# A new order of TensorE, ScalarE, VectorE and store instructions in a fused attention and feed-forward kernel on one core

## The chip, the core and the metric

The kernel runs on one core of a Trainium2 chip. A core has five engines with an instruction queue each: TensorE (PE in the profile, with its weight loads shown apart as PEld), ScalarE (ACT), VectorE (DVE), GpSimd (POOL) and SyncE (SP). Each engine takes its own queue in order, and semaphores make an instruction wait for work on another engine. TensorE writes its products to PSUM, and ScalarE or VectorE move them from there to the on-chip memory. DMA transfers are started by POOL's and SP's queues. The metric is the time of one execution on the device in microseconds.

## The reference

Eight batches b of 12 heads, 448 positions, 64 values a head. The attention has no softmax: scores are clipped at zero and squared. Its output is the input of a feed-forward layer with an exact GELU. Inputs and output are float32.

```python
scores = scale * np.matmul(q, k.transpose(0, 1, 3, 2))     # scale = 1 / sqrt(64)
attn = np.maximum(scores, 0.0) ** 2 / S                    # S = 448
attn_out = np.matmul(attn, v)                              # (8, 12, 448, 64)
x = attn_out.transpose(0, 2, 1, 3).reshape(B * S, H * D)   # (3584, 768)
h = x @ w_in                                               # w_in (768, 2048)
g = 0.5 * h * (1.0 + erf(h * inv_sqrt2))
out = g @ w_out                                            # w_out (2048, 768)
```

## The kernel before, in words

**Attention.** The 12 heads make three groups g of four. For each batch and group the kernel needs transposed keys (kT) and queries (qT). For the first two batches TensorE makes them: a TK step (L620) or a TQ step (L648) transposes into a PSUM bank `tp`, and one copy on ScalarE (L521) or VectorE (L519) brings the bank to kT or qT. For the later batches SP's queue makes them with transposing DMAs (L675), from natural-order data that POOL's queue loads (L472 to L477 for queries, L556 and L559 for keys, L579 for values, L492 to L494 and L498 for the two weight matrices). A QK step (L752) multiplies one block of 64 keys or two of them with the queries of four heads into a PSUM pair `ps`. Its relu follows on ScalarE (L769) or VectorE (L771), which empties the pair into a tile `a_sq`; the square of that tile is on VectorE (L781) or ScalarE (L779). When the seven key blocks of a group are squared, an AV step (L831) multiplies them with the values into a PSUM pair `pav`, and two copies empty it into xT, the transposed attention output. In the first batch, attention works in halves of 224 query columns, named a and b here, so that the pairs of the 128x896 relus hold two half blocks.

**Feed-forward.** Two forms of the first product exist. For the earliest part, psh steps (L891, with the GELU at L901) multiply xT by `win_sb` directly. For the rest, F1 steps (L1048) use a scheme with seven block products in place of eight, on sums of weight blocks (`ws`, L962), sums of activation blocks (`t_x`, L1007) and partial sums added by VectorE (L1086), with the GELU at L1098; FB steps (L1199) are the same for the last batch. The second product (F2, L1375) uses the same scheme, adds its parts at L1409, and the finished rows of 128 tokens go to the output by SP's queue (L1328).

**What sets the order.** Every step is registered as one `Op` in a list (`sch.open`), in an order that the program fixes. A string `ORDER` (L83 to L175, 1618 words) then names all of them once, in the order in which they are issued. The letter of a word is the engine: P and Q for TensorE, A for ScalarE, D for VectorE, G for POOL, S for SP; the number is the index in the list; Zn is a product of zeros over n columns on TensorE (L1677) that does nothing but fill time. `Scheduler.place` takes the words one by one:

```python
for word in ORDER.split():
    if word[0] == "Z":
        op, eng = next(fills), "PE"
    else:
        op, eng = self.open[int(word[1:])], names[word[0]]
        if word[0] == "Q":
            op.split()
    ...
    self.commit(max(self.ready(op), free), op, eng, dur, lat)
```

Since each engine has its own queue, only the order of the words of one engine among themselves, and the order in which words ask for buffers, reaches the chip. The number next to a QK step's is its relu and the one after that its square (P33, 34, 35); the two after an AV step's are its copies to xT (P45, 46, 47); the one after a TK or TQ step's is its copy (P17, 18).

**Buffers.** A step takes a buffer where its word stands and waits until an earlier owner has been read. There are three PSUM pairs (`w`), for QK, AV and F1 steps, two single PSUM banks (`f`), for TK, TQ, psh, fill and F2 steps, and 14 tiles `a` for relu outputs and partial sums. A word with Q in place of P takes the two single banks in place of a pair, and its relu becomes two instructions of half the size.

**Names that the text uses.** P14 and P17 are TK steps of batch 0, group 0 and P11 is its TQ step; P19 and P23 are the TK steps of groups 1 and 2. P33, P36, P39 and P42 are the first QK steps. P45, P60 and P72 are the AV steps of half a, P87, P99 and P114 those of half b. P165, P168, P171, P174, P198, P207 and P213 are QK steps of batch 1. P141 and P143 are the first two psh steps, P258 the first F1 step. P225 is an AV step of batch 1 and P375 an F1 step that reads its xT. P299 is the first QK step of batch 2. S1612 and S1613 are the last two stores (L1328): S1612 stores 256 of the last right half's 384 columns and S1613 the remaining 128.

Of the kernel before, what the change touches and what calls it, by code (L numbers as in the profile page):

```python
# [100 lines left out]
D423 P428 D456 D426 P459 A427 A424 D440 G234 A419 P311 P317 P445 P461 A441 D453 D449 D457 A318 D460  # L101
S230 S231 P463 P323 D312 A429 A381 A446 A313 D462 S232 P308 D316 S233 D301 A324 D309 D464 P350 P465
D466 A351 D352 P305 P302 A306 D310 P335 A307 P467 G237 G149 G152 G155 D458 D336 D468 A303 D304 P469
D470 P326 A327 P365 A366 P341 A342 D319 P471 P338 G239 G292 A339 A340 P320 D491 D472 A321 P332 A322
D337 D492 D343 G293 G294 D493 A333 P329 G295 D330 D367 S475 S476 P495 G296 A496 P497 P353 D498 P359
D334 D360 A331 A354 P362 A363 P499 S473 A500 P501 P356 P347 D325 A364 D328 P344 A357 A358 D355 D348
G297 D361 D345 D346 D349 G481 P511 A512 P520 A521 P503 P517 D502 A518 P526 P368 A369 D527 A519 P514
D504 S477 S478 G484 D494 S479 S480 P529 P505 D370 D583 P587 A513 P604 P507 D584 D515 G298 P594 A530
G487 A588 P589 A595 D605 D586 D522 A528 P607 P590 D508 D585 D592 P611 A516 P606 D608 A591 G482 G483
D621 D609 P599 A612 G485 G486 P596 S657 D531 P613 G488 D600 A601 S658 G489 S510 P623 P640 G663 D597  # L110
D614 P616 D617 A610 A641 A624 D622 P602 D506 P619 P625 P642 A593 A615 A603 A620 A598 Q523 D628 D645
A524 A646 P535 P626 P643 D525 S509 A536 A627 P630 P647 P538 A539 D631 D644 Q532 D533 A618 A534 P571
A572 P632 D648 P649 D673 P635 Q550 P553 A554 P652 D650 A651 D633 P638 P655 A656 D551 D674 A639 D636
A637 P677 P577 D653 A654 P559 A560 P547 S659 P679 D552 D675 P565 D548 S660 A678 D680 A578 A555 D540
P562 D563 D537 A566 S661 A567 D676 P681 P683 A682 D684 A634 P541 P574 P544 A545 D546 A629 A564 G666
P685 D686 S474 D542 D543 D693 D694 G490 P687 D688 S691 P689 D690 P568 A575 A549 A569 P556 D695 P719
A557 A558 A720 P713 D714 P697 D698 P725 A726 A727 A576 P728 D729 P722 D696 A570 P699 S692 D700 P731
P737 D732 P701 D702 D723 P703 P705 P746 D579 S662 G669 G664 G665 A561 D573 A747 P580 G667 A581 D704
D706 D730 D582 D785 P716 P709 A717 D710 S712 G668 G670 D786 P789 D788 G671 P806 A724 D790 P791 D794
D807 A738 P796 P813 D814 P707 A718 D787 A733 D715 P808 A739 D811 D708 A721 A812 P809 P792 D823 A810  # L120
P749 A750 Q734 D793 P740 A741 A795 D797 P798 P815 D816 P818 D819 D799 A742 A735 A736 D748 P825 P842
A843 P801 P821 P804 A751 A805 Q770 D802 P752 S711 A822 D826 P828 P845 A846 P832 D824 D753 D829 P849
D875 P827 S859 S860 S861 P844 D754 A850 P854 A800 S862 P834 P851 A771 A803 P879 D855 D830 D852 A833
D835 D847 P837 A817 A820 A853 P840 P857 P764 D876 D838 P755 D765 D877 A880 P883 A756 D878 A836 A858
A831 P773 A774 P761 D762 P881 D882 A841 G865 G868 A848 A884 P743 A763 A839 P767 D768 P918 D766 A775
P885 D886 P887 G672 D757 D888 A744 A856 A919 D745 P889 D890 D772 S893 P933 A934 D895 A935 P758 A759
D896 P779 A780 P776 A777 S863 A760 P891 P899 A900 S864 D898 P945 P927 D892 A778 P921 A922 A928 D946
D781 A947 P903 D920 P901 D897 P942 P948 A949 D769 D943 P782 A783 P924 G871 D902 A904 P930 D929 D931
D932 A925 P905 D906 A784 P907 D908 G866 P951 P915 D923 P939 D987 P909 G867 A940 D926 G869 G870 G872
D910 D988 P911 D912 S914 A952 P991 P1008 A916 A917 D990 Q963 D964 D944 P957 G873 A953 S1061 A958  # L130
D959 P936 A937 Q954 A938 P998 P1015 D992 P993 P1010 D1009 S1062 D989 A999 D950 P1011 A1016 A955
D1013 A1014 A956 P994 D996 P1003 D1012 A995 P1020 P1027 D1025 P1044 P1000 D1021 A1022 D1004 D1028
A1045 D1001 P1029 A997 P1046 D1049 A1050 D1032 A1005 P1030 P1047 D1026 P1017 D1018 A1031 P1034 P1051
D1048 S1063 S1064 S1065 A1002 P1023 P1036 P1053 D1052 D1054 A1035 D1037 P1039 P1056 P1006 G1067
A1007 G1070 D1057 D1079 A1024 P1042 P1059 A1060 P1081 D1040 S913 P978 A1041 A1043 A1058 P1117 D941
A979 P960 A961 D1077 D1078 D1118 P1150 D1151 S894 D962 P1120 P1083 A1121 P966 P972 A1082 P969 A973
P1085 P1141 D980 D967 D1084 A970 D1086 A968 D974 D1080 P981 A982 G874 A1055 P975 P1087 D1088 D1142
P1089 A1033 D1090 A976 P1091 A983 A1019 D1092 A1038 P1144 P1132 D1097 D977 P1147 A965 D971 A1133
A1148 D1134 P1093 P1101 D1094 S1095 S1066 P1129 A1130 P984 A1119 P1126 D1099 D1098 P1103 A985 A986
D1102 P1105 D1104 D1127 A1106 A1145 P1107 P1135 A1131 P1123 P1156 A1124 D1122 P1109 D1143 P1195  # L140
G1073 G1068 A1125 D1136 A1157 P1193 D1189 P1212 G1069 G1071 G1072 D1137 A1149 S1263 P1210 D1108
D1110 P1111 D1100 P1113 G1074 D1128 A1211 D1215 P1165 A1194 G1075 D1198 D1112 S1115 A1199 A1166
# [1572 lines left out]
```

## Time and profile before

| what | value |
|---|---|
| median of three runs | 359.96 us (359.49 to 360.23) |
| profiled execution, its own time | 360.24 us |
| its span in the profile | 358.5 us |
| TensorE busy | 350.0 us in 3841 matmuls |
| VectorE busy | 305.6 us in 515 instructions |
| ScalarE busy | 270.3 us in 437 instructions |
| POOL busy | 102.9 us in 138 instructions |
| DMA moved | 43.01 MB, mean 120 GB/s |

All times in the profile count from the start of the span. A row of a timeline has the start, the length from the start of its first instruction to the end of its last, the engine and line, the operation with output and input, the tile mode for TensorE, the sizes, and the number of instructions that the row joins; in brackets stands the idle time of the engine before it and what ended this. Instructions of one engine overlap by part of their length, so what a step costs its engine is read as the distance between starts. In the digit strip the span is cut in 40 slices of 9.0 us, and each digit is the busy share in tenths.

### The profile page before, as it was taken

How to read it: one execution, taken by the hardware profiler on the slowest of the kernel's cores; microseconds unless marked ns; L12 is line 12 of the kernel's file. 1: busy time of each engine (PE TensorE's matmuls, PEld its weight loads, DVE VectorE, ACT ScalarE, POOL GpSimd, SP SyncE). 2: the span in 40 equal slices, each digit the busy share in tenths (PEclk: the TensorE clock that was granted, in tenths of full speed). 3: DMA queues.
4: the chain of work that ended last, by engine and by line, in shares of the span. 5: the costliest groups of instructions: out<-in, count | busy, mean ns of one | idle time of the engine just before them, and what ended most of it. 6: DMA issues, size and time to landing. Idle time of an engine off the chain costs nothing.

```text
span 358.5 us, 9223 instructions
## 1 busy us (share of the span) xinstructions
PE 350.0 (98%) x3841; PEld 248.0 (69%) x3841; DVE 305.6 (85%) x515; ACT 270.3 (75%) x437; POOL 102.9 (29%) x138
## 2 busy tenths in 40 slices
PE   8879999999999999999999999999999999999995
PEld 3557679955588655896557965579668855788663
DVE  2999999999997989988889898779988998595762
ACT  3999997899869896978978669789986778334300
POOL 8664816096193104700075100841000000000000
PEclk9999999999999999999999999999999999999999
DMA  9999999999999958995399941998402001012222
GB/s 171 197 201 204 201 204 157 146 145 148 183 141 146 214 84 127 154 169 79 63 90 159 214 69 51 88 171 209 72 3 90 2 0 46 3 44 90 88 87 91
DMA packets 124361, 43.01 MB, mean 120 GB/s; under 512 B 102688, under 2 KB 120992, under 8 KB 124320
## 3 DMA queue, kind: packets, MB, share of 16 engines
q0 software_dynamic: 85328, 22.47, 66.2%
q1 hardware_dynamic: 38448, 19.50, 26.0%
q8 instruction: 30, 0.49, 0.5%
q10 hardware_dynamic: 544, 0.46, 0.4%
q14 instruction: 11, 0.09, 0.1%
HBM read 45.61 MB, written 11.01 MB: 158 GB/s over the span
## 4 chain that ended last, share of the span: by engine, by line
PE 92%; ACT 5%; DVE 2%; issue 0%; DVEq 0%; ACTq 0%
PE pso L1375 37%; PE pe L1048 30%; PE ps L752 9%; PE pav L831 8%; PE pb L1199 4%; ACT a_sq L769 3%; PE psh L891 2%; PE spin L1510 1%; DVE a_sq L781 1%; DVE a_sq L771 1%; ACT xT L521 0%; PE tp L620 0%; PE fill L1677 0%; ACT a_sq L779 0%; ACT qT L521 0%
## 5 line engine op out<-in xcount | busy, mean ns | idle before, releaser
L769 ACT ACTIVATE a_sq<-ps 128x896 bf16<-128x896 f32 (+1 forms) x125 | 106.7, 893 | 14.5 <-PE ps L752 14.2
L781 DVE TENSOR_TENSOR a_sq<-a_sq 128x896 bf16<-128x896 bf16 (+1 forms) x108 | 63.8, 615 | 2.1 <-ACT a_sq L769 1.9
L1375 PEld LDWEIGHTS <-s_sb 128*128 128x128 bf16 x456 | 42.4, 98 | 32.3 <-issue 7.1
L1048 PEld LDWEIGHTS <-win_sb 128*128 128x128 bf16 x624 | 59.5, 98 | 2.7 <-issue 1.5
L771 DVE TENSOR_SCALAR a_sq<-ps 128x896 bf16<-128x896 f32 (+1 forms) x57 | 55.5, 988 | 2.6 <-PE ps L752 2.2
L779 ACT ACTIVATE a_sq<-a_sq 128x896 bf16<-128x896 bf16 x61 | 57.2, 959 | 0.5
L752 PE MATMUL ps<-qT,kT 64*64 64x448 bf16 (+1 forms) x756 | 49.7, 337 | 2.7 <-ACT a_sq L769 1.3
L1098 ACT ACTIVATE h_sb<-part 128x448 bf16<-128x448 f32 x78 | 43.2, 580 | 9.9 <-DVE part L1086 9.7
L1086 DVE TENSOR_TENSOR part<-pe,part 128x448 f32<-128x448 f32 x78 | 45.5, 620 | 5.3 <-PE pe L1048 3.6
L1375 PEld LDWEIGHTS <-h_sb 128*128 128x128 bf16 x336 | 31.9, 98 | 22.9 <-issue 4.0
L1048 PEld LDWEIGHTS <-ws 128*128 128x128 bf16 x468 | 44.1, 98 | 3.5 <-issue 2.9
L1375 PE MATMUL pso<-wout_sb,s_sb 128*128 128x384 bf16 (+2 forms) x232 | 41.1, 321 | 0.0
L1375 PE MATMUL pso<-t_sb,s_sb 128*128 128x384 bf16 x224 | 41.1, 327 | 0.0
L1375 PE MATMUL pso<-wout_sb,h_sb 128*128 128x384 bf16 x224 | 41.1, 327 | 0.0
L559 POOL DMA_DIRECT2D nk<-in_k_dram x36 | 34.7, 968 | 9.6 <-DMA wout_sb<-in_moe_w_out_dram 8.1
L831 PE MATMUL pav<-a_sq,v_sb 64*64 64x448 bf16 (+1 forms) x756 | 36.5, 329 | 0.8 <-DVE a_sq L781 0.8
L752 PEld LDWEIGHTS <-kT 64*64 64x64 bf16 x756 | 19.6, 105 | 23.7 <-issue 17.7
L1048 PE MATMUL pe<-t_x,win_sb 128*128 128x224 bf16 x312 | 34.5, 259 | 0.0
L1048 PE MATMUL pe<-xT,win_sb 128*128 128x224 bf16 x312 | 34.1, 259 | 0.0
L1048 PE MATMUL pe<-t_x,ws 128*128 128x224 bf16 x312 | 33.2, 259 | 0.0
L521 ACT COPY part<-pe 128x448 f32<-128x448 f32 x53 | 26.4, 541 | 8.9 <-PE pe L1048 6.2
L1409 DVE TENSOR_TENSOR osb<-pso,p_sb 128x384 f32<-128x384 f32 x42 | 23.3, 554 | 9.4 <-PE pso L1375 5.9
(74 smaller groups left out, 409.5 us busy)
## 6 DMA issues: line engine op xcount, KB each, us to landing
out_dram<-osb SPq DMA_DIRECT2D x19, 384.0 KB, 2.8
nq<-in_q_dram POOLq DMA_DIRECT2D x38, 112.0 KB, 5.8
nk<-in_k_dram POOLq DMA_DIRECT2D x36, 112.0 KB, 5.8
v_sb<-in_v_dram POOLq DMA_DIRECT2D x5, 672.0 KB, 7.6
v_sb<-in_v_dram POOLq DMA_DIRECT2D x9, 224.0 KB, 8.0
win_sb<-in_moe_w_in_dram POOLq DMA_DIRECT2D x8, 192.0 KB, 9.2
wout_sb<-in_moe_w_out_dram POOLq DMA_DIRECT2D x4, 384.0 KB, 12.7
wout_sb<-in_moe_w_out_dram POOLq DMA_DIRECT2D x1, 1536.0 KB, 15.8
```

What stands on the lines that cost most here:

```text
L521: A.copy(dst, src)
L559: nc.gpsimd.dma_start(nk[b][:, g0, :, e], rows[:, e].rearrange("p (i d) -> p i d", d=D))
L752: nc.tensor.matmul(side(ps, e)[64 * j : 64 * j + 64, x * w : x * w + w], kT[r, g, i * 128 + 64 * j : i * 128 + 64 * j + 64], moving, start ...
L769: A.activation(to, x, AF.Relu, scale=c_att)
L771: V.tensor_scalar(to, x, c_att, 0.0, op0=mybir.AluOpType.mult, op1=mybir.AluOpType.max,)
L779: A.activation(ar, ar, AF.Square)
L781: V.tensor_mul(ar, ar, ar)
L831: nc.tensor.matmul(side(pav[0], e)[o2 : o2 + 64, :w], vt[b][r, 2 * g + e, bass.ts(i, D)], box["a2"][r, e, o : o + w], start=(i == 0), stop ...
L1048: nc.tensor.matmul(bank[name][:, y, z * HS : z * HS + HS], w[:, k, bass.ts(mm, 128)], right()[:, k], start=first and k == 0 and z == 0, st ...
L1086: V.tensor_add(get(to), ps(name), get(other))
L1098: A.activation(h_ring()[:, m : m + 2, o + half[c].start : o + half[c].stop], src().rearrange("p (x n) -> p x n", x=2), AF.Gelu,)
L1375: nc.tensor.matmul(box[bank][:, n0:n1], left()[:, kf], right()[:, kf, n0:n1], start=bool(need) and kf == 0, stop=kf == K2 - 1, skip_group_ ...
```

## The change

The string `ORDER` is written anew. It names the same 1618 operations, each once. Each engine keeps its number of words; 87 operations move from VectorE to ScalarE and 87 others from ScalarE to VectorE. POOL's words keep their order. The orders of TensorE, ScalarE, VectorE and SP differ. On TensorE, the first 74 places hold the same set of steps in both strings, in another order; after that (from P258) the orders differ locally. P39, P159, P225 and P550 are Q words before and P words after, and P72, P171 and P1117 from P to Q. On SP, 45 of the 67 words stand in another place, stores against transposing DMAs from batch 3 on, and at the end S1613 stands before S1612. Nothing else in the program is changed. The first lines, the line with Q299, and the last lines of both strings:

```diff
@@ -81,94 +81,94 @@
 ORDER = """
-G0 G1616 G1 G3 G4 G7 D13 Z1024 A10 G118 A16 G2 P14 D15 P11 D12 P17 D18 P19 D20 P42 A43 P36 A37 P33
-P21 D44 D22 P23 A24 D34 P51 P25 A52 D26 P48 Q39 D35 G117 P54 A49 D40 P63 A64 D55 P57 P27 D28 P29 D30
-P69 P66 A58 D59 P31 D32 A70 D71 A67 G121 G6 G125 D38 P90 P93 D41 A94 D65 P131 A132 P102 A103 P129
-P45 A46 A47 G126 Z672 A91 P84 D130 Q159 D50 D68 P72 G5 A160 D85 G8 G122 A73 G120 P111 A112 A53 D56
-D74 P75 P133 D76 P156 D113 A157 A134 P81 D82 P139 A140 P60 D61 D83 P96 P108 D62 A97 D109 P137 P78
-A79 D86 D80 P174 A175 D77 D92 P135 A136 D95 G124 P171 A172 D104 D98 P87 A88 P105 D89 A106 P168 A169
-P141 A142 P162 D107 D110 D138 P195 A163 P99 D100 Q114 G119 P207 D101 D176 P165 A196 A115 D116 A158
-P198 A199 D173 P143 A144 D208 D170 A166 D197 P240 A241 A161 D250 D251 P180 D181 D167 G128 G123 G9
-D164 P222 A223 P192 P242 A243 P244 D253 D209 P145 A193 A146 P213 A214 A245 D194 P177 A178 D200 P189
-A179 P183 D215 D190 D191 P246 A184 A247 P210 D182 A211 P216 P186 A187 D185 P248 A249 P258 P275 A217
-D254 G127 G236 D188 P219 A276 G235 G238 G147 A220 Q201 D224 D212 D255 G148 P204 A202 A203 A205 D252
-A221 P260 P277 A206 D259 P261 P278 A262 D409 D280 D218 D257 P265 D256 P282 A283 A266 Q225 A279 D412
-D263 P270 P267 A226 A227 D371 D372 P284 D268 A269 P287 D285 P375 A264 A281 P392 A393 P273 G150 D271
-P290 D288 P382 P399 D447 D374 A376 P378 P395 A274 D373 D450 A289 A291 D448 G151 P377 D451 P394 D397
-A286 A400 A383 P387 P404 D380 A396 A379 P384 A272 D405 A406 P401 D388 P413 P430 A389 A414 A431 D385
-A386 P420 P437 A421 D402 S228 A438 P407 D452 P390 D410 P416 A391 D411 P433 A408 D455 P442 S229 D454
...
-A417 A434 P415 A398 G153 G154 P432 D443 A444 D435 A436 D418 P422 P439 A403 Q299 A300 P314 A315 P425
...
-D1586 S1588 P1593 P1595 A1594 D1596 P1597 A1598 S1609 P1599 D1592 P1601 D1600 P1603 D1602 P1606
-S1610 D1604 S1611 P1605 D1607 S1612 D1608 S1613
+G0 G1616 G1 G3 G4 G7 D13 Z1024 A10 G118 P14 D15 G2 G117 G121 G6 P11 A16 P17 D12 P33 A18 P36 A37 G125
+D34 G126 P39 A40 P21 D22 P19 D20 P42 A43 P23 A24 D35 D38 P54 P48 A49 P25 D26 P57 A58 D41 Z672 D44
+P69 P27 D55 P29 A70 P66 D59 A30 P51 D28 A67 D52 G5 G8 P93 P31 P131 A94 D68 D132 P90 D32 A91 G122
+G120 G124 G119 G128 P63 A64 P84 D85 P129 A130 D65 P45 P133 D71 A46 A47 P108 P75 D134 A109 P78 A79
+D53 D76 Q72 A73 A74 D110 G123 G9 P102 A103 D50 P111 A112 P159 A160 G127 D56 P81 D82 A77 P139 D140
+P60 D95 D86 A61 A62 P156 A157 P137 P96 P141 D138 D104 A97 D98 A80 P168 P105 D83 A106 P135 D136 P87
+A142 A169 D92 D88 D89 P162 D113 Q171 A172 A163 D107 P174 P99 A100 D175 D170 D176 A101 Q114 A115 D116
+P195 D250 A196 D161 P213 A214 D215 P165 A166 D167 P143 A144 P240 P180 D158 A181 D173 A241 D197 P192
+A193 D164 P198 A199 D252 P244 A245 P242 D251 P222 D223 P207 A208 D182 A243 P177 A178 G236 P189 A200
+P183 A184 A179 P248 A249 D224 D190 D191 P246 A247 P186 P219 A220 G235 P210 A211 G238 G147 G148 D253
+P145 D209 P258 A146 D187 P275 G150 P216 D185 A212 D188 D194 Q201 A217 A259 D221 D254 D255 P204 A276
+A205 P260 P277 D257 A202 A218 D206 G151 D280 P261 D263 A281 D256 P265 P278 A279 P282 D266 P225 A262
+P267 P284 D409 D203 A283 A226 A227 P375 A376 P287 S228 S229 P270 D285 A286 D268 A269 P273 P290 A291
+D371 D372 P392 D288 A393 D271 D374 A272 P382 D412 A274 P399 G153 G154 P378 A400 P395 A289 D373 S230
+S231 S232 D450 D451 A383 P377 P394 D397 P387 A379 D388 A396 D380 P384 A381 A264 G234 P401 D402 D385
+A386 P404 D405 D410 D411 P413 P430 A431 P390 A414 D447 A391 P420 P437 A438 P407 G237 A408 D448 A421
...
+D449 P416 P433 A434 P415 S233 P425 A417 D426 P432 D435 P422 A389 A398 P442 A406 D418 G149 A427 Q299
...
+P1595 S1587 A1594 P1597 D1596 P1599 D1592 A1598 S1609 D1600 P1601 D1602 P1603 S1588 P1605 D1604
+S1610 S1611 P1606 D1608 S1613 D1607 S1612
 """
```

More of the change, by code (lines that the diff above doesn't have):

```diff
@@ L104 @@
[L104 to L118, printed above, removed]
@@ new lines @@
+P305 G296 P326 D466 D468 A340 D304 A306 D316 D327 P323 P469 D307 P471 D470 A419 S473 A444 D491 A324
+D492 P350 P329 A325 A330 P320 A321 G297 D472 A322 P362 D363 A351 P495 A496 D337 A352 A364 P332 D333
+P356 A357 P353 A354 D493 D334 S477 P497 D498 P499 D331 P501 D367 P359 A355 D328 A500 D358 P347 P344
+A348 D360 D361 D345 D346 P520 A521 S474 S478 P511 A512 S479 P503 D349 G481 G484 D502 P517 A518 P526
+D527 P368 A369 D370 D583 S480 D494 P529 A530 D531 G298 G487 G482 G483 G485 G486 P514 P505 D585 P587
@@ new lines @@
+P604 P589 A515 S657 P606 A513 D504 P507 D584 A528 P594 P611 D605 D609 A516 A588 D592 A593 D586 D506
+A595 A612 G488 P623 A624 P607 P590 D621 D508 S510 P599 P616 P640 A608 G489 D617 A591 A641 P613 A522
+P596 D600 D597 A598 D614 P625 P642 D645 P626 P643 D628 A618 P602 P619 D644 A601 D519 P630 D627 D622
+P647 D648 A610 D631 A646 A620 A603 A629 Q523 A524 D525 S658 P535 P632 A536 P649 D633 A615 D650 P652
+D653 P538 A539 D675 Q532 P571 A572 P635 A533 D673 A534 A654 D674 P638 D636 P655 A656 A637 A639 P577
@@ new lines @@
+D783 A784 D932 D906 D908 D950 P915 P939 D987 D988 A916 A917 P951 P909 D920 A940 P911 A923 A952 D910
+P991 P1008 D912 S864 Q963 D964 D990 S894 P957 A953 A958 D989 P936 A992 D937 D938 A1009 Q954 P998
+P1015 A965 A1016 P1011 D999 A1012 P993 P1010 D1013 D996 P994 D1025 A995 P1020 P1003 D1004 A1005
+P1000 P1027 P1044 D1021 A1022 D1001 A1002 D1028 D1045 P1029 P1046 D1049 A959 A1050 D1032 D1026 P1017
+A1014 A997 G871 G866 P1030 P1047 P1034 P1051 D1052 P1006 G867 G869 G870 G872 G873 A1031 A1048 P1036
+P1053 D1018 P1023 D947 A941 S913 D1054 A1035 D1037 A955 P1056 A1038 S1061 S1062 P1039 D956 A1024
@@ new lines @@
+A1007 D1079 D1040 P1042 P1059 Q1117 A1060 A1043 D1057 D1077 D1078 A1118 P960 A961 S1063 A1033 D962
+P972 D973 A1019 P1135 P1081 D1080 P1083 A1136 P975 S1064 S1065 A1082 D1084 A976 P981 D982 P978 A979
+P1085 A1055 G1067 G1070 D974 P969 S914 P966 D980 A967 P1141 D1086 P1087 P1144 D970 A1142 A1145 P1132
+P1150 D977 D983 P1089 D1088 P1091 D1090 A971 D1133 D968 A1041 D1092 D1146 A1058 P1093 D1094 P1147
+A1151 P1120 A1121 P984 G874 S1095 P1123 A1148 P1101 D1097 D1098 P1103 A985 A986 A1152 P1126 P1129
@@ new lines @@
+D1124 P1156 A1127 A1157 D1099 D1137 D1102 P1105 A1125 P1195 P1193 P1210 A1194 D1128 D1104 D1106
+P1212 D1100 P1107 P1109 D1211 A1122 D1215 A1216 D1198 A1119 D1108 P1111 D1110 A1130 D1112 D1131
+S1066 G1073 D1189 P1113 D1114 D1190 P1165 A1134 P1138 A1166 Q1153 D1192 A1154 D1158 G1068 G1069
+G1071 G1072 G1074 P1200 D1139 D1140 P1217 A1218 D1191 P1213 Q1177 A1201 P1159 A1160 P1196 D1227
+A1214 P1205 A1197 A1178 S1116 P1222 A1199 P1229 P1246 G1075 D1206 A1230 D1223 D1149 P1219 D1220
+P1231 P1248 A1207 A1247 D1234 P1202 D1203 P1232 P1249 A1224 D1251 P1208 A1161 P1236 A1235 D1250
@@ new lines @@
+P1253 A1155 A1221 P1225 A1204 D1228 D1233 A1226 D1237 P1238 D1239 A1240 S1263 P1241 D1242 A1252
+A1209 D1254 D1143 Q1168 S1096 P1244 A1243 P1255 D1256 S1264 S1265 S1266 A1169 P1258 S1267 D1259
+P1171 D1172 P1261 A1260 A1262 S1115 Q1174 A1245 D1175 P1162 A1257 D1269 D1270 A1163 P1295 A1164
+P1301 P1273 D1296 A1274 D1173 P1275 D1276 A1302 G1617 D1271 P1183 P1180 P1289 A1181 D1167 A1290
+P1277 D1278 P1279 A1184 A1182 P1281 A1185 D1179 P1307 A1308 A1303 D1176 D1170 D1272 D1280 D1282
+P1292 P1186 A1187 D1188 D1363 P1298 A1299 A1300 P1285 D1286 G1076 P1365 P1367 D1361 A1293 P1384
@@ new lines @@
+D1362 P1382 D1309 P1283 D1291 D1294 A1383 D1387 P1372 P1389 A1366 D1364 P1385 P1368 D1370 D1284
+P1304 A1373 A1390 D1369 A1371 Q1313 P1377 P1394 D1386 P1391 D1399 A1305 A1314 D1395 A1396 D1378
+P1401 P1418 D1419 P1403 P1420 A1388 D1306 A1402 D1406 D1423 A1297 A1379 P1374 D1375 A1376 P1404
+P1421 S1288 A1422 D1392 P1408 D1400 P1425 P1397 A1426 P1380 A1407 A1315 S1268 D1405 P1410 A1398
+D1409 P1427 D1428 D1411 P1413 P1430 A1381 P1340 A1429 A1341 D1431 Q1310 A1311 P1355 D1414 A1415
+A1432 D1356 P1328 A1329 D1312 D1435 P1416 P1433 A1434 P1439 P1346 A1417 P1349 A1347 P1325 A1350
@@ new lines @@
+D1436 P1441 D1438 A1440 P1337 D1326 D1475 P1319 A1320 D1442 A1393 P1322 P1443 D1437 P1445 A1323
+A1424 D1348 D1338 D1339 A1444 D1446 S1287 P1316 P1331 A1332 D1333 D1357 P1447 D1448 A1321 P1449
+D1450 A1412 A1351 D1455 D1456 A1324 D1330 P1343 A1344 P1352 A1353 P1451 D1452 S1454 A1354 P1459
+P1461 D1345 D1342 A1317 P1358 D1327 D1318 P1334 A1460 D1458 P1463 A1359 A1335 A1336 D1462 A1464
+D1457 D1360 P1481 D1479 D1477 D1478 P1465 S1453 D1476 P1489 D1466 P1483 P1498 A1482 P1500 P1467
+A1499 P1502 D1484 P1487 D1549 P1485 D1468 P1506 D1501 P1504 D1488 P1471 P1469 D1505 A1486 D1480
@@ new lines @@
+P1509 P1492 D1507 D1551 A1503 D1490 D1472 S1474 D1510 D1493 P1512 D1513 D1470 A1514 P1515 P1532
+A1533 P1517 A1511 P1534 D1535 P1495 D1496 P1553 P1523 P1540 A1516 A1491 D1518 P1538 P1519 P1521
+D1554 D1550 P1555 D1539 D1541 A1542 D1522 D1552 D1524 P1557 S1473 P1543 A1525 A1508 P1526 D1556
+P1559 D1527 A1528 A1520 D1544 A1497 A1494 D1558 P1546 D1547 A1548 P1561 A1545 D1560 D1562 P1529
+D1530 P1563 P1536 P1565 A1531 D1564 S1567 A1537 P1573 D1569 D1570 D1566 D1571 P1575 D1574 S1568
+P1577 D1576 A1578 D1572 P1579 D1580 P1581 D1582 D1591 P1583 D1584 P1585 P1593 D1589 D1590 D1586
```

72 lines of the change are left out of this document (18 added, 54 removed).

## The prediction

> **What bounds the kernel now.** I read the page first.
>
> ```profile
> span 358.5 us, 9223 instructions
> PE 350.0 (98%) x3841; PEld 248.0 (69%) x3841; DVE 305.6 (85%) x515; ACT 270.3 (75%) x437; POOL 102.9 (29%) x138
> PE   8879999999999999999999999999999999999995
> PE 92%; ACT 5%; DVE 2%; issue 0%; DVEq 0%; ACTq 0%
> ```
>
> TensorE is busy for 350.0 of 358.5 us, and the chain of waits is 92% TensorE. The change keeps every TensorE instruction, so only time in which TensorE waits can be won or lost. The digits put that time into the first four slices (36 us) and the last. The second view cuts the opening into stretches (columns: stretch, its length, then PE, PEld, DVE, ACT and POOL busy).
>
> ```profile
> 9.00:18.00 9.00, 7.59 (x196) 5.02 (x193) 9.00 (x19) 9.00 (x14) 5.62 (x9) 1.00 1.37 197
> 18.00:27.00 9.00, 7.12 (x200) 5.05 (x199) 8.96 (x16) 9.00 (x14) 5.50 (x9) 1.00 1.33 201
> 27.00:36.00 9.00, 8.75 (x160) 6.78 (x152) 8.79 (x18) 8.97 (x14) 4.61 (x7) 1.00 1.24 204
> ```
>
> From 9 to 27 us VectorE and ScalarE are busy 8.96 to 9.00 us of every 9, and TensorE 7.12 to 7.59. So the opening is bound by the two engines that empty PSUM. The waits of TensorE in 5 to 36 us say the same: none ends on a DMA.
>
> ```profile
> PE ps L752 <- ACT a_sq L769: 1.3, 4, 0.4
> PE pav L831 <- DVE a_sq L781: 0.8, 1, 0.8
> ```
>
> The timeline of TensorE shows which steps waited (start, length, what, idle time before it and its releaser).
>
> ```profile
> 24.48 0.38 PE L752 MATMUL ps<-qT,kT 64*64 64x448 bf16 x4 [0.27 <-ACT a_sq L769]
> ...
> 26.48 0.86 PE L831 MATMUL pav<-a_sq,v_sb 64*64 64x224 bf16 x28 [0.79 <-DVE a_sq L781]
> ...
> 27.72 0.38 PE L752 MATMUL ps<-qT,kT 64*64 64x448 bf16 x4 [0.18 <-ACT a_sq L769]
> ...
> 31.14 1.08 PE L752 MATMUL ps<-qT,kT 64*64 64x448 bf16 x12
> 32.15 2.47 PE L891 MATMUL psh<-xT,win_sb 128*128 128x224 bf16 x24
> ```
>
> Steps P174 (24.48), P87 (26.48) and P168 (27.72) wait. The row of 31.14 holds P207, P165 and P198, and takes 1.01 us to the next start for three steps of some 0.2 us each: a last wait. From 32.15 on TensorE has no such gap until the final products. **A microsecond taken out before P143 (32.15) reaches the end, if nothing later takes it back.**
>
> **How the work is counted.** In both lists I take a TensorE step, collect what it waits for (operands, and the release of the PSUM pair or bank that it takes), follow that back, and add up on each engine all that is queued up to the last piece needed, as an engine takes its queue in order. The price of a piece is start to start in a row without gaps.
>
> ```profile
> 10.06 5.81 ACT L769 ACTIVATE a_sq<-ps 128x896 bf16<-128x896 f32 x7
> ```
>
> ```profile
> 9.22 1.08 DVE L771 TENSOR_SCALAR a_sq<-ps 128x896 bf16<-128x896 f32 x1
> 10.22 0.38 DVE L519 COPY qT<-tp 128x448 bf16<-128x448 bf16 x1
> 10.52 0.62 DVE L781 TENSOR_TENSOR a_sq<-a_sq 128x896 bf16<-128x896 bf16 x1
> ...
> 14.54 2.23 DVE L781 TENSOR_TENSOR a_sq<-a_sq 128x896 bf16<-128x896 bf16 x4
> 16.67 0.62 DVE L519 COPY kT<-tp 128x896 bf16<-128x896 bf16 x1
> 17.21 1.16 DVE L781 TENSOR_TENSOR a_sq<-a_sq 128x896 bf16<-128x896 bf16 x2
> ```
>
> A relu costs ScalarE 0.80 to 0.81 ((5.81 - 0.95) / 6) and VectorE 1.00 (9.22 to 10.22); on VectorE a square costs 0.53 (14.54 to 16.67 for four), a whole kT copy 0.54, a small copy 0.30. ScalarE's other prices are differences of starts in its own rows:
>
> ```profile
> 15.65 1.02 ACT L521 COPY qT<-tp 128x896 bf16<-128x896 bf16 x1
> 16.43 1.06 ACT L769 ACTIVATE a_sq<-ps 128x896 bf16<-128x896 f32 x1
> 17.24 0.74 ACT L521 CAST xT<-pav 128x224 bf16<-128x224 f32 x2
> 17.70 1.97 ACT L769 ACTIVATE a_sq<-ps 128x896 bf16<-128x896 f32 x3
> ...
> 20.02 1.17 ACT L779 ACTIVATE a_sq<-a_sq 128x896 bf16<-128x896 bf16 x1
> 20.86 1.14 ACT L769 ACTIVATE a_sq<-ps 128x896 bf16<-128x896 f32 x1
> ```
>
> A full transposed copy costs 0.78 (15.65 to 16.43), an xT copy 0.23 (17.24 to 17.70 for two), a square 0.84 (20.02 to 20.86). The rest is scaled by columns.
>
> **The change, part by part.** (1) *The opening, ScalarE.* Before, P198 is the worst step: it needs 13 paired and 7 whole relus (16.0), 5 full transposed copies (3.9), 2 single relus (0.9), 1 square (0.8), 1 gelu (0.4), 4 xT copies (0.9), 2 casts (0.9): 23.9 us. In the new list the worst is P165, with one QK step (0.20) less of TensorE work ahead: 14 paired and 5 whole relus (15.2), 2 full and 2 smaller transposed copies (2.4), 2 squares (1.7), 8 xT copies (1.8), and the same single relus, gelu and casts (2.2): 23.3. Ahead of P165 both lists put 55 TensorE steps of the same kinds. With unrounded prices the gain is 23.90 - 0.20 - 23.27 = 0.43 us.
>
> (2) *The opening, VectorE.* P165 before: 19 squares (10.2), 7 relus (7.0), 6 small qT copies (1.8), 3 whole and 2 partial kT copies (2.2), 6 xT halves (1.8), 2 small squares and a cast (0.9): 23.9. Worst in the new list: P213, one QK step earlier, with 18 squares (9.6), 7 relus (7.0), 5 small and 3 full qT copies (3.1), 3 whole and 1 partial kT (1.9), 2 xT halves (0.6), and the same 0.9: 23.2. Gain, unrounded, 23.91 - 0.20 - 23.19 = 0.52. The smaller of the two counts: **0.43 us**.
>
> (3) *The first scores come earlier.*
>
> ```profile
> 5.26 0.51 ACT L521 CAST nk<-k 128x384 bf16<-128x384 f32 x1
> 8.04 1.35 ACT L769 ACTIVATE a_sq<-ps 128x448 bf16<-128x448 f32 x2 [2.27 <-PE ps L752]
> ```
>
> ScalarE idles for 2.27 us until the first scores. At 10.06 it has done 2.95 us of work: it runs 7.1 us behind the clock. The new list sends P33, P36, P39 straight behind P17 (before, P19's transposes stand between) and gives ScalarE A18, the kT copy behind P17. By hand: P17 ends near 7.2, A18 fills 7.3 to 7.7, P36 is done near 7.85, and A37 starts at 7.9 with 1.3 us of work done: 6.6 behind. Followed further the next relus find their scores in time up to 14 us. ScalarE's head start is thus 7.1 - 6.6 = 0.5; VectorE's, likewise, 6.8 - 6.6 = 0.2. Bounds: 0 (the idle time returns at a later wait) to 0.5. I take **0.5**, as the last binding step is ScalarE's; with VectorE binding instead it is 0.5 + 0.2 = 0.7 in all. The opening together: 0.43 + 0.50 = **0.93 us won**.
>
> (4) *Array changes.* TensorE passes between 64*64 and 128*128 products 114 times instead of 112.
>
> ```profile
> 108.98 1.31 PE L1048 MATMUL pe<-t_x,win_sb 128*128 128x224 bf16 x12
> 110.13 1.31 PE L1048 MATMUL pe<-xT,win_sb 128*128 128x224 bf16 x12
> 111.37 0.57 PE L752 MATMUL ps<-qT,kT 64*64 64x448 bf16 x8
> ```
>
> Twelve matmuls take 1.15 us before twelve of their kind and 1.24 before scores: 0.09 a change, 0.19 for two: **0.2 us lost**.
>
> (5) *Engines swapped.* 87 pieces move from VectorE to ScalarE and 87 back; net, ScalarE takes 10 relus more and VectorE 9 squares more. Behind P258 TensorE's own queue covers them: at equal TensorE pace the tightest direct chain is 0.1 to 0.2 us early in both lists. One is new: P375 follows AV P225 by two products (1.15 us from the rows above) instead of four, and needs two xT copies; I take 0, bounds 0 to 0.5. Three steps become Q (two banks in place of a pair) and four cease to be: two half-size relus for one, no price.
>
> (6) *Stores and transpositions.* POOL's queue is the same in both. SP's differs in 45 of 67 places, all of them store against transposition from batch 3 on. The last two stores change places, so a 128 KB store ends the kernel instead of a 64 KB one:
>
> ```profile
> out_dram<-osb SPq DMA_DIRECT2D x1, 128.0 KB, 1.7
> out_dram<-osb SPq DMA_DIRECT2D x1, 64.0 KB, 1.6
> ```
>
> 0.1 us at most; I take 0.
>
> What is late next is batch 2, whose transpositions follow landings that the change does not move:
>
> ```profile
> L675 SPq DMA_TRANSPOSE qT<-nq x1: 1246/1246/1246, 60.4 to 60.4; - x1
> DMA to landing us min/median/max: 8.0/8.0/8.0
> ```
>
> ```profile
> 69.90 0.57 PE L752 MATMUL ps<-qT,kT 64*64 64x448 bf16 x8
> ```
>
> Queries land at 68.4, the first scores of batch 2 (Q299) start at 69.9: at most 1.5 us can be won ahead of them; 0.93 passes.
>
> **The sum.** -0.93 + 0.19 = -0.74 us against the profiled execution's own 360.24 (358.5 span and 1.7 around it). The median of the runs shown, 359.96, is 0.3 lower; I put the same difference on it: **359.2 us**. One run differs from the next by 0.7 us (359.49 to 360.23), so 0.2%, 0.72 us, is about what can be told from no change; my value stands on that edge.
>
> **The rivals.**
> *The head start is eaten.* A wait that ends earlier may only meet the next. For it: P168 at 27.72 waits for the end of 20.0 us of ScalarE's pieces, so its distance behind the clock grew from 7.1 at 10.06 to about 7.5: holes come back. Against it: they are in before too, and (1) and (2) do not rest on the first scores. Then -0.43 + 0.19 = -0.24: 359.7, up to 359.9.
>
> *Three pairs bind, not the order.* TensorE's waits end on relus that give a PSUM pair back (1.3 us in four, above). If the round trip of three pairs sets the pace, any order has the same holes: 0 + 0.19, 360.1. For it: these four waits. Against it: ScalarE and VectorE are full in the same slices, so a fourth pair would wait for the same engines, and both lists empty a pair with the same kinds of pieces. The Trainium skill, "Perfetto Trace Analysis", section Optimization Strategy, says that a gap repeating on the engine that should be saturated can mean too little PSUM for the next tile; by that rule the time would be 360.1, and the trace agrees with the gaps but shows no idle engine behind them.
>
> *More is won.* Everything counted on both engines up to P258 is 69.9 us in the new list and 71.5 in the old; halved over two engines that is 0.8, and with ScalarE's 0.5 it is 1.3, below the 1.5 of batch 2. Then -1.3 + 0.19: 358.8.
>
> *Slower: ScalarE's queue stands still behind xT copies.* Up to P165 it takes 8 of them instead of 4, with relus queued behind each, and each needs its AV product. The view of waits over the whole span has this kind of wait (total, times, longest):
>
> ```profile
> ACT xT L521 <- PE pav L831: 4.6, 10, 0.8
> ```
>
> At 0.8 a copy, four more cost up to 3.2 us; a full ScalarE passes all of it on to P165. It decides from 1.4: there the gain of 0.74 has become a loss of 0.2%, and two late copies are enough. For it: ScalarE has no idle time in 9 to 27 us to absorb a wait. Against it: none of the ten lies in 5 to 36 us, and before takes four such copies there without a wait. Then -0.74 + (1.4 to 3.2) = 360.7 to 362.4, say 361. The Trainium skill, "PSUM — Partial Sum Buffer", section Engine vs sequencer instructions, calls these queues strict FIFO; the trace agrees, as ScalarE's pieces start in the order of its list.
>
> **How the numbers follow.** Forecast 359.2 (358.9 to 359.6): 0.38. More is won, 358.9 and below: 0.24. Head start eaten: 0.09. Pairs: 0.05. Slower, 360.7 and above: 0.24. Of the first case a little over half, 0.21, and all of the second lie below 359.24 (0.2%): faster 0.45. The rest of the first, the third and the fourth: same 0.31. Slower 0.24. The range leaves out the upper half of the slow rival (0.12) and 0.04 below: 358.5 to 361.0; the likeliest case alone has 358.7 to 359.7.
>
> **What would show it.** Part (3): the first whole relus on ScalarE and VectorE start before 8.0 and 7.8 us, and ScalarE's gap of 2.27 us is split by a kT copy. Parts (1) and (2): the first psh product (P141) comes some 4 us earlier than 28.03, P143 starts near 31, and the F1 product P258 starts about 0.9 before 43.90. Part (4): starts past P258 keep that lead but for 0.2 us. If P258 leads and the end does not, a later wait took it back: batch 2's scores waiting for qT, or P375 for xT. If TensorE's waits in the opening end on ScalarE for over 2.5 us in sum, the slow rival holds. A first wait that ends on a DMA would break the premise.

## The result: 0.19% slower

The new kernel takes 360.78 us (median of 12 runs, 359.82 to 361.96) against 360.13 before (12 runs, 359.49 to 360.23). The ratio is 1.0019, with a 95% interval of 1.001 to 1.0028: 0.65 us are lost where 0.74 were to be won. The profiled execution took 360.56 us (360.24 before). The page after:

```profile
span 358.7 us, 9221 instructions
PE 350.1 (98%) x3841; PEld 247.7 (69%) x3841; DVE 303.1 (84%) x512; ACT 269.6 (75%) x439; POOL 103.7 (29%) x138
PE   7989999999999999999999999999999999999995
PE 93%; DVE 3%; DMA 1%; ACT 1%; issue 0%; DVEq 0%
```

Little in it tells the two kernels apart; TensorE's first digits differ. The stretches of the opening (columns as before: stretch, length, then PE, PEld, DVE, ACT and POOL busy) show TensorE 0.5 us busier in each of 9 to 18 and 18 to 27 us, and 0.4 less from 27 to 36:

```profile
9.00:18.00 9.00, 8.12 (x220) 5.81 (x217) 9.00 (x17) 9.00 (x15) 5.57 (x9) 1.00 1.38 199
18.00:27.00 9.00, 7.59 (x183) 5.13 (x179) 9.00 (x16) 9.00 (x17) 5.55 (x9) 1.00 1.32 202
27.00:36.00 9.00, 8.36 (x153) 6.71 (x153) 8.33 (x17) 8.46 (x15) 4.61 (x7) 1.00 1.24 204
```

ScalarE and VectorE, full from 9 to 27 us, are idle for 0.5 to 0.7 us after that. The view of TensorE's waits in 5 to 44 us has, ahead of the relus, a line that the kernel before does not have:

```profile
PE pav L831 <- issue: 1.0, 1, 1.0
PE ps L752 <- ACT a_sq L769: 0.6, 1, 0.6
```

"Issue" means that TensorE waited for nothing that the profile shows. The timeline has this wait in the middle of AV step P87, behind nine of its 28 matmuls, and then P143 and P258:

```profile
26.00 0.47 PE L831 MATMUL pav<-a_sq,v_sb 64*64 64x224 bf16 x9
27.43 0.67 PE L831 MATMUL pav<-a_sq,v_sb 64*64 64x224 bf16 x19 [0.95 <-issue]
...
31.22 2.47 PE L891 MATMUL psh<-xT,win_sb 128*128 128x224 bf16 x24
...
43.16 1.02 PE L1048 MATMUL pe<-xT,win_sb 128*128 128x224 bf16 x9
```

P258 comes 0.74 us before its old 43.90. That is at equal work, 717 matmuls ahead of it in both kernels, although the first 74 places do not hold quite the same set of steps: P216 stands there before, P219 in the new list, both QK steps. But the last full product (P1603) starts later than before. First the row of before, then that of the new kernel:

```profile
352.07 1.46 PE L1375 MATMUL pso<-t_sb,h_sb 128*128 128x384 bf16 x8
```

```profile
352.25 1.46 PE L1375 MATMUL pso<-t_sb,h_sb 128*128 128x384 bf16 x8
```

So 308.17 us from P258 to P1603 have become 309.09: **0.92 us are lost behind the opening.** The views of waits name nothing there, as every gap is short. I took each TensorE step's distance to the next start, less the usual distance for that pair of kinds of step. Behind 43 us the new kernel exceeds it by more than 0.04 us at twelve places, 1.03 us in sum; the kernel before does at two places, 0.25. One of the twelve, six matmuls at 55.27 that take 0.70 us in place of 0.58 (half of the 1.15 for twelve):

```profile
55.27 0.74 PE L1048 MATMUL pe<-xT,win_sb 128*128 128x224 bf16 x6
55.97 0.75 PE L1048 MATMUL pe<-t_x,ws 128*128 128x224 bf16 x6
```

On VectorE, in the same time:

```profile
53.74 0.50 DVE L1007 TENSOR_TENSOR t_x<-xT 128x672 bf16<-128x672 bf16 x1
54.34 0.51 DVE L1007 TENSOR_TENSOR t_x<-xT,t_x 128x672 bf16<-128x672 bf16 x1
54.76 1.15 DVE L1086 TENSOR_TENSOR part<-pe,part 128x448 f32<-128x448 f32 x2
```

The second addition of the last row gives back the PSUM pair that P382 takes at 55.97. Its product was done at 54.28; it stood in VectorE's queue behind two activation sums and another addition, until 55.91. In nine of the twelve the last release comes from VectorE. Without its like in the kernel before, the sum is 1.03 - 0.25 = 0.78. The trace has 102 array changes behind P258 in place of 100; at the forecast's 0.19 for two the sum would be 0.97, against the 0.92 seen.

### The profile page after: what moved, and what is told of

It reads as the page before. It is cut to its first block, busy times and chain, and to the rows that moved or that the text cites. A ratio compares the mean times of both kernels' runs of the same rounds, so it can differ in the third digit from the quotient of the medians.

```text
span 358.7 us, 9221 instructions
## 1 busy us (share of the span) xinstructions
PE 350.1 (98%) x3841; PEld 247.7 (69%) x3841; DVE 303.1 (84%) x512; ACT 269.6 (75%) x439; POOL 103.7 (29%) x138
## 4 chain that ended last, share of the span: by engine, by line
PE 93%; DVE 3%; DMA 1%; ACT 1%; issue 0%; DVEq 0%
PE pso L1375 37%; PE pe L1048 30%; PE ps L752 10%; PE pav L831 9%; PE pb L1199 4%; PE psh L891 3%; DMA k<-in_k_dram 1%; DVE a_sq L771 1%; DVE a_sq L781 1%; ACT a_sq L769 1%; DVE qT L519 0%; PE tp L620 0%; ACT xT L521 0%; PE tp L648 0%; DVE kT L519 0%
## 5 line engine op out<-in xcount | busy, mean ns | idle before, releaser
L769 ACT ACTIVATE a_sq<-ps 128x896 bf16<-128x896 f32 (+1 forms) x137 | 114.1, 879 | 15.1 <-PE ps L752 14.3
L781 DVE TENSOR_TENSOR a_sq<-a_sq 128x896 bf16<-128x896 bf16 (+1 forms) x117 | 68.8, 615 | 3.1 <-ACT a_sq L769 2.8
L779 ACT ACTIVATE a_sq<-a_sq 128x896 bf16<-128x896 bf16 x52 | 49.1, 961 | 0.3
L771 DVE TENSOR_SCALAR a_sq<-ps 128x896 bf16<-128x896 f32 (+1 forms) x44 | 44.4, 1021 | 4.4 <-PE ps L752 4.3
L521 ACT COPY part<-pe 128x448 f32<-128x448 f32 x57 | 28.5, 538 | 11.8 <-PE pe L1048 8.9
```

The costliest lines, as they stand in the source:

```text
L521: A.copy(dst, src)
L769: A.activation(to, x, AF.Relu, scale=c_att)
L771: V.tensor_scalar(to, x, c_att, 0.0, op0=mybir.AluOpType.mult, op1=mybir.AluOpType.max,)
L779: A.activation(ar, ar, AF.Square)
L781: V.tensor_mul(ar, ar, ar)
```

## The experiments

Times stand beside those of the kernel before in the same series, 360.1 to 360.2 unless another is named. A lead or a start is that of the one profiled execution. The length of a stop is given from one start to the next; the idle time in the brackets of a row is some 0.2 to 0.3 us shorter.

**Which part loses.** Two mixtures, joined at P258.

```diff
 e1: words of the new list up to P258, then the words of before that are left, in their order
 e2: words of before up to P258, then the words of the new list that are left, in their order
```

> New list up to the first F1 step (P258), then the words of before in their order. Theory (the opening gives 0.74 us, the rest of the new list takes 0.93 back: 0.19 in two more array changes, 0.67 in eleven short waits of TensorE): 0.74 under before, 359.4, and the lead of 0.74 at P258 is still there at the last product. Rival (the new opening is itself no gain over many runs, since its stall in the middle of AV step P87 varies): within 0.3 of before or above it. A second rival (a lead in the opening is taken back anyway by batch 2's late queries): 0 to -0.2, with a wait before P299.

> Words of before up to P258, then the words of the new list in their order. Theory: nothing is won in the opening and the rest takes 0.93, so 361.0 to 361.1, 0.9 above before, with about eleven short waits of TensorE behind 43 us. Rival (the opening costs, not the rest): as before within 0.3.

e2 took 361.21, 1.05 more than before (ratio 1.003, 1.0018 to 1.0043). Its profile has the waits of the new list at nearly the same steps (0.62 us in nine behind 43 us), so they do not hang on the new opening. But the 1.05 is not all theirs: from P143 to P258 e2 takes 12.34 us in place of 11.75, and one QK step more, of some 0.2 us, explains only a part of that. e1 took 360.67 (ratio 1.0004, 0.9991 to 1.0018): not the 359.4 of the theory. Nine runs lie at 360.64 to 360.95 and three at 359.46 to 359.70; the profile is of the three. In it P14 starts at 5.01 us, against 5.86 in the new kernel and 5.93 before. The joint also costs something of its own: P258 waits 0.20 for a relu, and P204 and P1538 are late by 0.29 and 0.17, there and in the two other kernels joined this way (e4 and e6), and in neither parent. The new opening alone is thus no clear gain here, and with 0.66 us lost at the joint e1 does not tell what it is worth.

**Are the short waits a matter of a few places in the queues?** (e3)

```diff
-D674 D636 | D576 D688 | D876 D878 D855 | D742 D762 | A953 A958 | D1228 D1233 | D1306 D1406 D1423 | D1400 D1405
+D636 D674 | D688 D576 | D855 D876 D878 | D762 D742 | A958 A953 | D1233 D1228 | D1423 D1406 D1306 | D1405 D1400
```

> The new list with ten words moved back by one to three places in their own engine's queue (sums, squares and partial sums that are not due for 1 us or more), so that eight pieces on which TensorE waited come ahead of them. Theory (these waits carry the loss): their 0.58 us goes, so 0.4 to 0.6 under the new list, 360.2 to 360.4. Rival (the loss is in the array changes and in a slower pace, and each removed wait only makes the next one longer): 0.2 or less is won, 360.6 and above.

360.83, as the new kernel: the rival's time and its longer waits hold. Five waits were gone, but P1413 now waited 0.25, P1011 0.11, P885 0.09 and P918 0.17 in place of 0.13: 1.07 us in sum, as ever. This fits a VectorE that is late as a whole at these places, so that a piece that is let ahead makes the next one late; no run shows that directly. The next run (e8) changes engines, not places.

```diff
-P283 A283 D203 A200 ...   (behind P258: engines as in the new list)
+   each of 148 words behind P258 with the letter that before gives it, places unchanged
```

> The new order, but behind P258 each relu, square, copy and partial sum on the engine that before gives it (148 words change between ScalarE and VectorE). Theory (the short waits behind P258 come from the new split, which lets VectorE's queue run late): the waits over 0.04 us fall from about 1.0 to 0.3 to 0.5 us in sum and the time to 360.2 to 360.4. Rival (they come from the places of TensorE's steps, with pieces too close behind them): waits of 0.8 us or more, 360.7 or above.

399.08 us, far more than either theory was about. Its profile has TensorE waiting 3.5 us for VectorE's relus, 3.4 each for its copies and additions, 3.3 for ScalarE's relus. Order and split are one plan: the test does not tell which of the two makes the waits of the new kernel, and this stays open.

**The stop in P87.** Every kernel so far with the new opening has it, and always behind 478 matmuls from the start of the program (1.21, 0.58 and 1.44 us in the new kernel, e1 and e3). The page of the new kernel has the transfers that bring instructions (queue and kind, number, MB, share):

```profile
q8 instruction: 30, 0.49, 0.5%
```

For 3841 matmuls that is one transfer for 128 matmuls with their weight loads. The Trainium skill, "Runtime: NRT & Kernel Launch", section Instruction fetch mechanics, says that an engine's instructions are streamed in 16 KiB blocks of 256 and that crossing a block's end is mostly hidden. The trace agrees with the size of the blocks (0.49 MB in 30); the runs below show that crossing a block's end is not hidden here. In the traces one such transfer starts 2.4 to 2.6 us ahead of the end of each of these stops. Four runs (e4 to e7) move the work against the blocks.

> As the first run, with psh step P141 (12 long matmuls) moved from ahead of P168 to directly ahead of P87, and its gelu one place back. TensorE stands still for 0.95 us in the middle of P87 in the new kernel while no semaphore holds it, 2.4 us after an instruction load began. Theory (the next instructions had not arrived): the long matmuls fill this time, the stall in P87 is below 0.4 us and P258 starts 0.3 to 0.7 earlier than in the first run, the time 358.7 to 359.1. Rival (P87 waits for its operands, or the stall is bound to no place): P258 no earlier than in the first run, the time 359.4 or above.

```diff
-P137 P96 P141 D138 ... P135 D136 P87 A142 A169
+P137 P96 D138 ... P135 D136 P141 P87 A169 A142
```

In e4 the stop stayed, 0.95 us, behind 478 matmuls, P258 came at 44.22 in place of e1's 43.09, and the time was 360.78: the long products ahead of it did not help, as the load itself began only at 25.34 us.

```diff
-    for _ in range(SPIN):
-        nc.tensor.matmul(spin[:, 0, :], zero, zeros, start=True, stop=True)
+    for n in [NB] * 6 + [69] * 22:
+        nc.tensor.matmul(spin[:, 0, :n], zero, zeros[:, :n], start=True, stop=True)
```

> The new kernel with 28 warm-up products (L1510) in place of 9, in all as many columns as before, so that every later TensorE instruction stands 38 places further back in its stream. In the four kernels with the new opening seen so far TensorE stops without a semaphore after exactly 478 matmuls. Theory (a block of its instructions, about 128 matmuls with their weights, arrives 2.4 us after its load begins, and ends there): it now stops, if at all, 19 matmuls earlier in the work, in P135, behind the 12 long matmuls of P141, for 0.3 us or less; P87 runs through, P143 starts 0.3 to 0.8 earlier than 31.2 to 31.7, and the time is 0.3 to 0.6 under the new kernel: 360.2 to 360.5. Rival (P87 waits for something of its own): the stop stays in P87 and the time at 360.8.

> The same 28 warm-up products with the new opening and the words of before behind P258 (first run of this study, 360.67). Theory: 0.3 to 0.6 less, 360.1 to 360.4. Rival: 360.7.

P87 ran through in both, so its operands were not what it waited for. But TensorE now stopped behind 351 matmuls, in Q72 (0.73 us in e5 and 1.27 in e6), and the times were 361.30 and 361.28: the stop moved and nothing was won. The row of e5:

```profile
19.81 0.29 PE L831 MATMUL pav<-a_sq,v_sb 64*64 64x224 bf16 x3 [0.47 <-issue]
```

In the trace of e5 P258 starts at 43.10, no later than in the new kernel (43.16); what is lost there in addition is a wait of batch 2's scores for their queries, which landed at 70.09 in place of 68.27, the cap that the prediction named:

```profile
PE ps L752 <- DMA qT<-nq: 0.8, 1, 0.8
```

**The same on the old order** (e7). With `[NB] * 3 + [68] * 45` warm-up products:

> The kernel before, its order untouched, with 48 warm-up products of as many columns in all, so that the ends of the instruction blocks fall 39 matmuls earlier in the work: at 312 (P111), 439 (P135) and 567 (in AV step Q114), where 36 matmuls ahead take only some 1.1 us. Theory (the old order lost little because its block ends fell where TensorE waited anyway or ran long matmuls): stops without a semaphore at the same counts of matmuls, the time 0.4 to 1.2 over before, 360.6 to 361.4. Rival (the position of instructions means nothing): 360.15 within 0.2.

361.41, 1.27 us over before, by a change that adds no column to TensorE's work. Three stops without a semaphore, behind 351, 479 and 607 matmuls:

```profile
20.07 0.44 PE L752 MATMUL ps<-qT,kT 64*64 64x224 bf16 x9 [1.03 <-issue]
...
26.27 0.41 PE L648 MATMUL tp<-ident,nq 112*64 112x112 bf16 x9 [0.55 <-issue]
...
32.46 0.28 PE L831 MATMUL pav<-a_sq,v_sb 64*64 64x224 bf16 x1 [0.33 <-issue]
```

The stops end 6.20 and 6.19 us apart. From 20 to 32 us the opening here runs at the pace at which TensorE is handed its instructions.

**A shift between two blocks** (e9). The filling products Z672 move to where TensorE waits for a relu, as 17 small ones.

```diff
-P57 A58 D41 Z672 D44 ...   P159 A160 G127 D56 P81
+P57 A58 D41 D44 ...        P159 A160 G127 D56 Z672 P81
-            for x in range(0, n, NB):
-                c = min(NB, n - x)
+            w = 40 if n == 672 else NB
+            for x in range(0, n, w):
+                c = min(w, n - x)
```

> The new kernel with its filling products Z672 moved from 11 us to directly ahead of P81, where TensorE waits 0.6 us for a relu, and cut into 17 products of 40 columns. The block end after 351 matmuls stays in P81 (two places back), the one after 478 moves back by 15 matmuls, from P87 into P135, behind the long matmuls of P141. Theory (the stop in P87 is the block end): no stop over 0.3 us in P87, P143 0.5 to 1.0 earlier than 31.2 to 31.7, the time 0.3 to 0.9 under the new kernel: 359.9 to 360.5, less where batch 2's queries (landing at 68.3 to 70.1 in the profiles) take part of it back. Rival (VectorE and ScalarE bind there anyway and the stop only fills a wait): P143 at 31.2 to 31.7 as before, 360.8.

P87 ran through, but the stop was 1.06 us long at 478 matmuls, now in P135, and P143 started at 31.25 although P14 had started 0.7 us earlier than in the new kernel. The time was 361.31, with 360.55 for before in this series (ratio 1.0016, 1.0000 to 1.0032). The stops end at 20.60, 26.72 and 32.86, at 351, 478 and 606 matmuls, 6.1 apart. Both the expected gain and the rival's reason fell: VectorE and ScalarE are busy for only 7.80 and 8.64 us of the 9 from 18 to 27 us, so it is the blocks that set the time here.

```profile
20.60 0.56 PE L1678 MATMUL fill<-zero 64*64 64x40 bf16 x13 [0.78 <-issue]
...
26.72 0.34 PE L648 MATMUL tp<-ident,nq 112*64 112x112 bf16 x6 [0.85 <-issue]
```

**A joint at Q299** in place of P258, alone (e10) and with the moved filling products (e11):

> The new list up to the first scores of batch 2 (Q299, 69 us), then the words of before. Theory (0.75 of the 0.93 lost behind P258 is lost behind 69 us: eleven of the twelve waits, and the array changes): 0.6 to 0.8 under the new kernel, 360.0 to 360.2, with waits behind 69 us of 0.25 as in before. Rival (the loss hangs on the lead, not on the new words: any list that comes early waits): 360.6 to 360.9.

> Both edits together: the new opening up to Q299 with the filling products ahead of P81, then the words of before. Theory: the gains add up but for what batch 2's queries take back, 359.2 to 359.9, under both kernels. Rival (the queries' landing at 68.3 to 70.1 takes all of it back): 360.0 to 360.4 with a wait of 0.3 us or more ahead of Q299.

363.97 and 365.55. P428 waited 2.51 us and P459 0.87 right behind the joint, for VectorE and ScalarE pieces of before's list that were issued too late there. The two say nothing on the question they were made for.

**Why the blocks are late.** From 12 to 35 us the DMA engines also bring w_in. Left out, on the kernel before (e12), the new one (e13) and e7 (e14):

```diff
-        nc.gpsimd.dma_start(t[0], w[0])
+        nc.gpsimd.memset(t[0], 0.0)
     ... and so for the two other loads of L492 to L494
```

> The kernel before with the loads of w_in (6.3 MB, 12 to 35 us) left out; GpSimd writes zeros in their place, so its output is all zeros and only its times count. Control for the next run: in before no block end stops TensorE, so P143 stays at 31.9 to 32.2 and the time at 359.8 to 360.3, if the loads bind nothing there.

> The new kernel with the loads of w_in left out in the same way. Theory (TensorE's instruction blocks come late because the bulk loads are ahead of them): the stop in P87 after 478 matmuls falls below 0.4 us and P143 comes 0.5 to 1.0 earlier than 31.2 to 31.7; the time is 0.3 to 0.9 under the new kernel. Rival (a block takes its 2.4 us from the start of its load whatever else is moved): the stop stays at 0.9 to 1.4, P143 at 31.2 to 31.7, the time as the new kernel.

> The kernel before with 48 warm-up products, which stopped at 351, 479 and 607 matmuls for 1.31, 0.76 and 0.58 us, 6.2 us apart, now without the loads of w_in. Theory (the loads delay the blocks): the three stops together below 1.2 us, the resumptions less than 6.0 apart, and the time 0.5 to 1.2 under that run. Rival (cadence of its own): stops of 2.3 to 2.8 in sum, 6.1 to 6.2 apart, no gain in time.

| | with w_in | without |
|---|---|---|
| before | 360.13 | 360.25 |
| new | 360.78 | 359.75 |
| before, 48 warm-up products | 361.41 | 360.38 |

The kernel before does not feel the loads; the medians of the other two are 1.03 us higher with them. Against the kernel before in its own series the ratios without them are 0.9982 (0.9969 to 0.9995) for the new order and 1.0006 (0.9994 to 1.0017) with the 48 products, and against e12 the new order is 0.50 us ahead by medians, at the edge of what ten runs of each (359.57 to 361.75 and 359.39 to 360.41) can tell. In the new kernel without the loads P87 runs through, and P143 and P258 start at 31.02 and 42.96, though P14 starts as late as 5.94:

```profile
26.55 0.88 PE L831 MATMUL pav<-a_sq,v_sb 64*64 64x224 bf16 x28
...
31.02 1.23 PE L891 MATMUL psh<-xT,win_sb 128*128 128x224 bf16 x11
...
42.96 1.12 PE L1048 MATMUL pe<-xT,win_sb 128*128 128x224 bf16 x10
```

In before without them P258 starts here:

```profile
43.80 1.03 PE L1048 MATMUL pe<-xT,win_sb 128*128 128x224 bf16 x9
```

The lead is 0.84 us. P143 itself comes only 0.20 earlier than with the loads, not the 0.5 to 1.0 expected: a QK step now waits 0.43 us for a relu at 28.54, P14 starts 0.08 later, and a block's end is still felt once, behind 351 matmuls, where P81 starts 0.29 us after the end of the relu that it waits for (0.06 in the new kernel) and 2.45 us after a load began. Behind P258 0.90 is lost again (309.06 against 308.16 us to P1603; first the row of e12, then that of e13):

```profile
351.96 1.30 PE L1375 MATMUL pso<-t_sb,h_sb 128*128 128x384 bf16 x7
```

```profile
352.02 1.30 PE L1375 MATMUL pso<-t_sb,h_sb 128*128 128x384 bf16 x7
```

These two executions agree with that: they took 360.26 and 360.41. But 360.41 is the highest of e13's ten runs; where an execution at their median gains the rest of the 1.03 us over the new kernel no trace here shows, and this stays open.

With the 48 products, the stops of 1.31, 0.76 and 0.58 become one of 0.90. In e7 five instruction loads in a row start 6.1 to 6.3 us apart (11.57 to 36.30); in e14 the first two still start 6.0 apart, the next 3.4, 5.5 and 5.4. So the w_in loads delay the instruction blocks, and a cadence that the blocks keep by themselves is excluded from the third block on. What spaces the first two, and whether it is the moving of w_in or the issuing of its loads by GpSimd that holds up the others, these runs do not tell.

## Why the prediction was wrong

- **What bounds the kernel now** held only in part. TensorE's gaps of the opening do lie in the first 32 us, and "a microsecond taken out before P143 reaches the end, if nothing later takes it back" was sound. That the opening is bound by the two engines that empty PSUM holds for before, and for the new order up to 27 us, where both are still busy for 9.00 of 9. But in P87, which the new order reaches 0.48 us earlier, TensorE meets another bound, the instruction blocks. No row of before showed it, since there TensorE is at or behind each block's end when the block comes.
- **Parts (1) to (3), 0.93 won in the opening.** The signs came true: ScalarE's gap is split by a kT copy at 7.18 us, the first whole relus start at 7.71 and 7.52, P141 at 23.73 in place of 28.03, P143 at 31.22. The size is 0.84 where the blocks come nearly in time (e13 against e12). With the stop it was 0.74 in the profile, and 0.22 in another execution of the same opening (e3, P258 at 43.68). The stop was 0.6 to 1.4 long and its length is not the order's to choose. The rival "the head start is eaten" was right that a lead can meet a later wait, but this wait is for instructions, not for an engine.
- **Part (4), two array changes, 0.19 lost**: the two changes are there. Their price was not measured by itself; the 0.92 us lost less the 0.78 of the waits leaves 0.14 for them.
- **Part (5), "I take 0": the step that failed.** "At equal TensorE pace the tightest direct chain is 0.1 to 0.2 us early in both lists" took a slack of 0.1 to 0.2 us as enough to cover every release. Measured: twelve waits, 1.03 us, in place of two, 0.25. P375, the one place that the prediction named, did not wait. The loss is a trait of the words behind P258, not of the lead: from P258 to P1603 the new list takes 309.06 to 309.11 us in the new kernel, e3, e9, e13 and, without its wait of 0.89 for queries, e5, and the list of before 308.16 or 308.17 in before, e7, e12 and e14, wherever P258 starts (42.96 to 44.99). Why the slack was not there, by the places or by the engines of the pieces, stays open (e3 and e8).
- **Part (6)** and the cap at batch 2: stores and transpositions cost nothing seen; the cap bound in e5, not in the new kernel.
- **The rivals.** "Slower: ScalarE's queue stands still behind xT copies" had the sign and not the mechanism: ScalarE never waits for an AV product in 5 to 36 us. That 360.78 lies inside the stated 358.5 to 361.0 is luck, as the upper part of that range was there for this rival alone. "Three pairs bind" finds no support: the opening moved by 0.84 with the same pairs.

The sum as it should have been: -0.84 (opening), of which the stop takes some 0.1 to 0.6, +0.19, +0.78. That is +0.2 to +0.7; 0.65 was measured, 0.32 in the profiled pair. As the loss behind P258 is the same in five traces of the new list, a loss of 0.65 by medians would leave the opening a lead of some 0.3 us (an estimate, 0.92 - 0.65), less than half of the 0.74 in the profiled run.

## What to carry to other kernels

Where TensorE has no gaps left, pieces on ScalarE and VectorE that come just in time can turn into many short waits under a new order (here twelve, 1.03 us in sum, none of which a view of waits names); a slack of 0.1 us per release is a price, not a zero. Where small matmuls run beside bulk loads, count matmuls: at every 128th the instructions themselves can be late, and splitting the warm-up products, 39 more of them with no column more, cost 1.27 us. Look for "issue" in the waits of TensorE before an opening is put down to its operands.

## What was not expected of the hardware

In these runs TensorE stops at fixed counts of matmuls (351, 478 or 479, 606 or 607), for 0.4 to 1.4 us, with no semaphore, wherever the work stands; the load of the next block starts 2.2 to 2.6 us ahead of the resumption. With the w_in loads beside them, blocks that bind come 6.1 to 6.2 us apart in e7 and e9, so that TensorE gets no more than some 21 matmuls a us there. Behind 36 us no such stop over 0.3 us is seen in any trace: twelve 128x224 matmuls take 1.15 us there, half that pace.
